# A transformer block on one Trainium2 core: arithmetic of the gated stage on VectorE instead of GpSimd, given out in smaller steps

## The chip, the cores and the metric

One core of a Trainium2 chip runs the kernel. The metric is device time in microseconds (us) of one execution; lower is better. The engines are called as the profile calls them: PE (TensorE, matmuls), DVE (VectorE), ACT (ScalarE), POOL (GpSimd), SP (SyncE, which issues nearly all DMAs). Each works through its own instructions in order and waits where one needs another engine's or a transfer's result.

## The reference

A block with adaptive layer norm, attention with a compressive memory, and a gated bilinear unit. S = 2048 rows, D = 512, 32 heads of 16, F = 1376:

```
mod = silu(c) @ w_mod                                  # six vectors sa, ca, ga, sb, cb, gb
h = layernorm(x) * (1 + ca) + sa
x = x + ga * attention(h, wq, wk, wv, wo, beta)        # four segments of 512 rows
h = layernorm(x) * (1 + cb) + sb
x = x + gb * (((h @ w_gate) * (h @ w_up)) @ w_down)    # the gated stage
```

Everything is f32, and the change lies in the last two lines.

## The kernel before

The attention part takes about 520 us. It is written out as one hand-made order of PE work, with generators that are advanced a step at a time between the matmuls, so that the preparation of later work is spread under them. The gated stage begins as the attention ends.

**Precision.** Each f32 operand of a matmul is split in a high part (rounded by ACT, `activation(..., AF.Copy)` into an `fp32r` tile, whose name ends in H or h) and a low part (operand minus high part, a subtraction, name in L or l). A product is three matmuls: high by high, high by low, low by high. A "six" is such a product over two blocks of 128 along the inner dimension: six matmuls of 128 x 512 (function `six`, matmul at L1260).

**Two passes.** Pass 0 does segments 0 and 1, pass 1 segments 2 and 3. F is cut into eleven tiles f of 128 (the last of 96). Tiles 0 and 1 of pass 0 and the last tile are multiplied directly (`open0`, `close0`, `other`; names Xg, Xu, Yg, Yu, q).

**Units.** The other tiles go in pairs (i, i + 1), first for w_gate ("g"), then for w_up ("u"). A unit computes the 2 x 2 block product (two tiles of F by two segments) with seven block products instead of eight, by sums of weight blocks and differences of blocks of h. `unit` runs them in the order 2, 5, 1, 3, 6; products 7 and 4 are carried into the next unit (`tail`). PSUM banks Z, Y and X hold the sums. ACT copies a bank out (p5, p1, y, L1369), DVE adds one bank to such a copy (`add`, L1349: p1g, yg, p5g, yu, p5u, and so on), and PE goes on writing bank X only when DVE has read it. At the end of a u unit DVE multiplies gate by up (`finish`, L1345), and `split` makes mH on ACT (L1279) and mL on DVE (L1280). `down` multiplies these with w_down (PE L1317, "acc") and DVE adds the result to the row tile (L1320, "xa"); eight such products per pair stand in the queue `dq` and are taken at fixed steps.

**Preparation.** `prepare(n)` prepares unit n, two units ahead: `wprep` loads the raw weights (cr), makes four sums of blocks S (tile cs, L479 to L483) and high and low parts of seven blocks (cwH by ACT L487, cwL by POOL L488). In three steps at the end of `wprep` each high part is followed by its low part. Units of pass 0 store cwH and cwL to DRAM (`keep`); pass 1 loads them back (`fetch`) and ACT rounds them again (L416), except for its last two units, which come from raw weights. For a u unit `wdprep` loads two tiles of w_down (crd), multiplies them by gb (L1295) and splits them (L1296, L1297). `xprep` splits the last tile's weights (cwL-1, L436). `build(p)` makes the blocks of h and their differences (`comb`, tile t, POOL L1224), each with high part bH (ACT L1216) and low part bL (DVE L1217). `lnC(s)` does the norm of segment s: statistics (L565), 1/sqrt(v + eps) by Ln and Exp on ACT with one correction step on four numbers per row (POOL L581 to L585, for s = 1 on DVE), the scaling of four row tiles x (L588), the transposes by PE, and the copies by ACT (L597).

**Order.** In the gated stage the order of PE is fixed by hand: each matmul depends on the one before it (`pe`). Other instructions are placed by a scheduler when the kernel is built; `pin` keeps one behind the last PE instruction. The driving loop takes one step of `prepare` at each of the six steps of a unit:

```
    for n in range(NU):
        pr = prepare(n + 2)
        ...
        for st in (unit if nm != "x" else x_unit)(n):
            next(pr, None)
            ...
        run(pr)
```

Of the kernel before, what the change touches and what calls it, by code (L numbers as in the profile page):

```python
# [8 lines left out]
F32 = mybir.dt.float32  # L9
# [48 lines left out]
def tile_kernel(ctx, tc, x, wq, wk_, wv, wo, beta, w_gate, w_up, w_down, c, w_mod, out):  # L58
    nc = tc.nc
# [359 lines left out]
    def xprep(n, tag, pool, rpool):  # L419

        wh = pool.tile([P, 7, 2, P], F32R, tag=f"wh{tag}", name=f"cwH{n}", bufs=1)
        wl = pool.tile([P, 7, 2, P], F32R, tag=f"wl{tag}", name=f"cwL{n}", bufs=1)
        m = ft[LAST][1]
        for j, nm in enumerate("gu"):
            plain[int(n == CH), LAST, nm] = wh[:, 0:4, j], wl[:, 0:4, j]
        flat = [a.rearrange("p a b c -> p (a b c)")[:, 0:8 * P] for a in (wh, wl)]
        if n == CH:
            yield from fetch(("x", LAST), flat, wkeep)
            return
        raw = rpool.tile([P, KT, 2, P], F32, tag="raw0", name=f"cr{n}", bufs=1)  # L430
        nc.gpsimd.memset(raw[:, :, :, m:], 0.0)
        for j, w in enumerate((w_gate, w_up)):
            pin(nc.sync.dma_start(raw[:, :, j, 0:m], w.rearrange("(k p) f -> p k f", p=P)[:, :, LAST * P:]))
        yield
        act.activation(wh[:, 0:4], raw, AF.Copy)
        nc.gpsimd.tensor_sub(wl[:, 0:4], raw, wh[:, 0:4].bitcast(F32))  # L436
        yield
        keep(("x", LAST), flat, wkeep)
        yield
# [19 lines left out]
    def wprep(n, tag, pool, rpool):  # L459

        _, nm, i = units[n]
        if (nm, i) not in wkeep:
            raw = rpool.tile([P, KT, 2, P], F32, tag=f"raw{(n + 1) % 2}", name=f"cr{n}", bufs=1)
        wh = pool.tile([P, 7, 2, P], F32R, tag=f"wh{tag}", name=f"cwH{n}", bufs=1)
        wl = pool.tile([P, 7, 2, P], F32R, tag=f"wl{tag}", name=f"cwL{n}", bufs=1)
        wslot[n] = wh, wl
        if (nm, i) in wkeep:
            yield from fetch((nm, i), [a.rearrange("p a b c -> p (a b c)") for a in (wh, wl)], wkeep)
            return
        views = [w.rearrange("(k p) f -> p k f", p=P)[:, :, i * P:] for w in (w_gate, w_up)]  # L470
        gp = nc.gpsimd
        pin(nc.sync.dma_start(raw.rearrange("p k r c -> p k (r c)"), views["gu".index(nm)][:, :, 0:2 * P]))
        yield
        S = rpool.tile([P, 4, 2, P], F32, tag="ws0", name=f"cs{n}", bufs=1)

        def A(r, c):
            return raw[:, 2 * c:2 * c + 2, r]

        gp.tensor_add(S[:, 0], A(1, 0), A(1, 1))  # L479
        gp.tensor_sub(S[:, 1], S[:, 0], A(0, 0))  # L480
        yield
        gp.tensor_sub(S[:, 2], A(0, 0), A(1, 0))
        gp.tensor_sub(S[:, 3], A(0, 1), S[:, 1])  # L483
        yield
        top = raw[:, :, 0].rearrange("p (c k) f -> p c k f", c=2)
        for d, v in ((slice(4, 6), top), (6, A(1, 1)), (slice(0, 4), S)):
            act.activation(wh[:, d], v, AF.Copy)  # L487
            gp.tensor_sub(wl[:, d], v, wh[:, d].bitcast(F32))  # L488
            yield

    def wo_load(s, pool):
        rw = []
# [61 lines left out]
    def lnC(s, pool, hpool, xpool, tag, nb, bk):  # L554

        xt = []
        for t in range(4):
            a = xpool.tile([P, D], F32, tag=tag, name=f"x1_{s}_{t}", bufs=nb)
            pin(nc.sync.dma_start(a, x1d[s][t]))
            xt.append(a)  # L560
        yield 0.1
        mv = pool.tile([P, 4, 2], F32, tag="mv", name=f"cmv{s}", bufs=2)
        for t in range(4):
            st = pool.tile([P, 6], F32, tag="st", name=f"cst{s}_{t}", bufs=2)
            pin(vec.bn_stats(st, xt[t]))  # L565
            vec.bn_aggr(mv[:, t, :], st)
            yield 0.0
        sd = pool.tile([P, 4], F32, tag="sd", name=f"csd{s}", bufs=2)
        act.activation(sd, mv[:, :, 1], AF.Ln, bias=epst[:, 0:1])
        y = pool.tile([P, 4], F32, tag="y", name=f"cy{s}", bufs=2)  # L570
        act.activation(y, sd, AF.Exp, scale=-0.5)
        a = pool.tile([P, 4], F32, tag="ya", name=f"cya{s}", bufs=2)
        b = pool.tile([P, 4], F32, tag="yb", name=f"cyb{s}", bufs=2)
        if s == 1:
            vec.tensor_mul(a, y, y)
            vec.scalar_tensor_tensor(b, mv[:, :, 1], EPS, a, op0=ALU.add, op1=ALU.mult)
            vec.tensor_scalar(b, b, -0.5, 1.5, op0=ALU.mult, op1=ALU.add)
            vec.tensor_mul(y, y, b)
        else:
            eng = nc.gpsimd  # L580
            eng.tensor_mul(a, y, y)  # L581
            eng.tensor_scalar(b, mv[:, :, 1], 1.0, EPS, op0=ALU.mult, op1=ALU.add)
            eng.tensor_mul(b, b, a)
            eng.tensor_scalar(b, b, -0.5, 1.5, op0=ALU.mult, op1=ALU.add)
            eng.tensor_mul(y, y, b)  # L585
        yield 0.0
        for t in range(4):
            pin(vec.tensor_scalar(xt[t], xt[t], mv[:, t, 0:1], y[:, t:t + 1],  # L588
                                  op0=ALU.subtract, op1=ALU.mult))
            yield 0.0  # L590
        for d in range(KT):
            if d % 2 == 0:
                hfs[s, d // 2] = hpool().tile([P, 2, L], F32, tag=f"hf{s % 2}{d // 2}", name=f"chf{s}_{d // 2}", bufs=1)
            ps = bk(f"ctp{s}_{d}")
            for t in range(4):
                TP(ps[:, t * P:(t + 1) * P], xt[t][:, d * P:(d + 1) * P], ident)
            act.activation(hfs[s, d // 2][:, d % 2], ps, AF.Identity, scale=cb_c[:, d:d + 1], bias=sb_c[:, d:d + 1])  # L597
            if s == 0:
                if d % 2 == 0:
                    pieces[0, 1 + d // 2] = tuple(hpool().tile([P, 2, L], F32R, tag=f"b{x}{1 + d // 2}", name=f"b{x}0_{1 + d // 2}", bufs=1)  # L600
                                                  for x in "hl")
                hi, lo = (a[:, d % 2] for a in pieces[0, 1 + d // 2])
                h = hfs[0, d // 2][:, d % 2]
                act.activation(hi, h, AF.Copy)
                nc.gpsimd.tensor_sub(lo, h, hi.bitcast(F32))
            yield 0.45
# [602 lines left out]
    def build(p):  # L1209

        def emit(j, srcs):
            pool = bc if j < 3 else pc
            hi = pool.tile([P, 2, L], F32R, tag=f"bh{j}", name=f"bH{p}_{j}", bufs=1)
            lo = pool.tile([P, 2, L], F32R, tag=f"bl{j}", name=f"bL{p}_{j}", bufs=1)
            for k in range(2):
                pin(act.activation(hi[:, k], srcs[k], AF.Copy))  # L1216
                pin(vec.tensor_sub(lo[:, k], srcs[k], hi[:, k].bitcast(F32)))  # L1217
            pieces[p, j] = hi, lo

        T = pc.tile([P, 2, L], F32, tag="ws1", name=f"t{p}", bufs=1)  # L1220

        def comb(a, b):
            for k in range(2):
                nc.gpsimd.tensor_sub(T[:, k], a[k], b[k])  # L1224

        t = [T[:, k] for k in range(2)]
        b11, b12, b21, b22 = ([hfs[2 * p + c, r][:, k] for k in range(2)] for r in range(2) for c in range(2))
        if p > 0:
            emit(2, b21)
            yield  # L1230
        comb(b12, b11)
        yield
        if p > 0:
            emit(1, b11)
            yield
        emit(5, t)
        yield
        emit(3, b22)
        yield
        comb(b22, t)  # L1240
        yield
        emit(6, t)
        yield
        comb(b21, t)
        yield
        emit(4, t)
        yield
        comb(b22, b12)
        yield
        emit(7, t)  # L1250
        yield
# [31 lines left out]
    def wdprep(p, f, tiles=None):  # L1283
# [10 lines left out]
        yield  # L1294
        vec.tensor_mul(r, r, gbb)  # L1295
        act.activation(hi, r, AF.Copy)  # L1296
        vec.tensor_sub(lo, r, hi.bitcast(F32))  # L1297
        yield
        keep(("d", f), (hi, lo), dkeep)
# [198 lines left out]
    for w in wdp[:2]:  # L1498
        next(w)
    run(open0(0, LAST, qa[LAST]))  # L1500
    next(wdp[2])
    next(nb)
    next(pr0)
# [34 lines left out]
    for n in range(NU):  # L1538
# [4 lines left out]
        if n == CH - 1:  # L1543
            nb = build(1)
        for st in (unit if nm != "x" else x_unit)(n):
            next(pr, None)
            if n == 0:
                next(pr1, None)
                next(nb, None)
            if n == 0:  # L1550
                d(1 + st % 2 if st > 1 else 1)
            elif st in DS[nm] and n < NU - 1:
                d()
            if 1 <= n < CH - 1:
                next(lg, None)
            if n in (CH - 1, CH):
                next(nb, None)
# [37 lines left out]
```

## Time and profile before

| | |
|---|---|
| time, median of 3 runs | 901.0 us (899.87 to 902.4) |
| profiled execution | 900.34 us, of which the profile's span is 898.6 us |
| mean granted TensorE clock | 0.99 |
| PE busy from 725 to 898.6 us | 166.48 of 173.60 us |
| DMA | 141.29 MB, mean 157 GB/s |

How to read the rows shown below. A row of the page's first part gives, for each engine, busy time, share and number of instructions. A row of stages gives the stretch, its length, busy time (and number of instructions) of PE, PEld, DVE, ACT and POOL, then the granted TensorE clock as a share of full speed, the mean share of time that the DMA engines were busy, and GB/s. A group row gives line, engine, operation, output<-inputs, shapes and count, then busy time and the mean duration of one in ns, then idle time just before these instructions and what ended it. A timeline row gives start, duration, engine, line, operation and count, and in brackets the idle time before it and what ended it. A row without a bracket waited for nothing. Instructions of an engine overlap a little: the next one starts before the one ahead has ended.

### The profile page before, as it was taken

What the parts mean: (1) busy time and instruction counts of PE and PEld (TensorE: products, weight loads), DVE (VectorE), ACT (ScalarE), POOL (GpSimd) and SP (SyncE); (2) the same over time, 40 slices, a digit from 0 to 9 for tenths busy, and PEclk for the clock granted to TensorE, in tenths of its full rate; (3) what the DMA queues carried; (4) which work ended last, traced back from release to release, by engine and by line L of the source; (5) the groups of instructions that cost most, each with busy time, mean ns of one, the idle gap of its engine ahead of it and who ended that gap; (6) DMA issues with size and microseconds to landing.
All of it is one profiled execution on the core that took longest, in us unless ns stands there. A gap on an engine that the chain in (4) does not pass through costs nothing.

```text
span 898.6 us, 14447 instructions
## 1 busy us (share of the span) xinstructions
PE 852.6 (95%) x4975; PEld 600.1 (67%) x4976; DVE 647.0 (72%) x1720; ACT 496.7 (55%) x745; POOL 389.3 (43%) x521
## 2 busy tenths in 40 slices
PE   8989999999999999999999989997899989999998
PEld 5755656556665566666666666866688768888876
DVE  8698777888788877878886368884946945545544
ACT  3758767687676865777455453252434744554420
POOL 4546536565464763856235446493550300004200
PEclk9999999999999999999999999998999999999999
DMA  7555335454454545465674484763543566443012
GB/s 235 146 160 154 109 105 143 141 156 131 128 138 128 154 145 133 120 181 177 191 216 130 153 284 153 245 258 129 211 162 132 189 232 196 180 154 124 27 48 93
DMA packets 83305, 141.29 MB, mean 157 GB/s; under 512 B 11712, under 2 KB 45504, under 8 KB 83232
## 3 DMA queue, kind: packets, MB, share of 16 engines
q1 hardware_dynamic: 83088, 140.35, 49.6%
q8 instruction: 39, 0.64, 0.3%
q14 instruction: 34, 0.28, 0.1%
q10 hardware_dynamic: 144, 0.02, 0.0%
HBM read 90.52 MB, written 49.55 MB: 156 GB/s over the span
## 4 chain that ended last, share of the span: by engine, by line
PE 71%; DVE 15%; ACT 6%; DMA 2%; issue 2%; POOL 2%; SPq 1%; ACTq 0%; DVEq 0%; POOLq 0%
PE acc L1317 13%; PE tb L85 7%; PE q L85 6%; PE k L85 6%; PE Xg L1260 6%; DVE q L39 5%; PE Xu L1260 5%; PE wops L85 4%; PE vps L85 4%; PE Yg L1260 4%; PE Yu L1260 4%; PE kps L85 3%; PE qps L85 2%; ACT pt L332 2%; PE Zu L1260 1%
## 5 line engine op out<-in xcount | busy, mean ns | idle before, releaser
L39 DVE CUSTOM_DVE_ANT_0 q<-q,cmask 128x384 f32<-128x384 f32 (+3 forms) x512 | 246.5, 508 | 49.1 <-PE q L85 39.1
L332 ACT ACTIVATE pt<-k 128x1024 f32<-128x1024 f32 x160 | 163.8, 1024 | 64.4 <-PE k L85 63.7
L338 POOL TENSOR_SCALAR_AFFINE_SELECT pt<-pt 128x256 f32<-128x256 f32 (+1 forms) x224 | 97.3, 449 | 166.4 <-ACT pt L332 164.0
L85 PE MATMUL q<-kst,qst 96*128 96x384 bf16 (+3 forms) x512 | 101.5, 299 | 11.1 <-DVE nm L39 9.8
L1320 DVE TENSOR_TENSOR xa<-xa,acc 128x512 f32<-128x512 f32 x96 | 65.3, 683 | 59.0 <-PE acc L1317 58.8
L85 PE MATMUL k<-qst,kst 98*128 98x384 bf16 (+3 forms) x512 | 97.1, 302 | 5.0 <-ACT pt L332 4.9
L85 PE MATMUL tb<-pt,v 128*32 128x512 f32 (+3 forms) x1024 | 75.5, 436 | 0.0
L39 DVE DVE_READ_ACCUMULATOR2_ANT nm<- 128x1 f32 x512 | 72.1, 141 | 0.0
L85 PEld LDWEIGHTS <-kst 98*128 98x128 bf16 x512 | 37.7, 98 | 49.5 <-issue 43.5
L85 PEld LDWEIGHTS <-qst 96*128 96x128 bf16 x512 | 43.2, 97 | 37.7 <-issue 13.6
L1317 PE MATMUL acc<-dH,mH 128*128 128x512 f32 (+1 forms) x152 | 60.8, 400 | 3.0 <-ACT mH L1279 3.0
L1317 PE MATMUL acc<-dH,mL 128*128 128x512 f32 (+1 forms) x152 | 60.3, 397 | 3.1 <-DVE mL L1280 3.1
L1317 PE MATMUL acc<-dL,mH 128*128 128x512 f32 (+1 forms) x152 | 60.3, 397 | 0.0
L479 POOL TENSOR_TENSOR cs<-cr 128x256 f32<-128x256 f32 x10 | 8.6, 856 | 107.2 <-DMA cr<-in_w_gate_dram 102.3
L85 PEld LDWEIGHTS tb<-pt,v 128*32 128x32 f32 x1024 | 28.7, 109 | 38.6 <-issue 34.4
L364 ACT ACTIVATE tsb<-tb 128x512 f32<-128x512 f32 x32 | 19.0, 595 | 41.0 <-PE tb L85 41.0
L488 POOL TENSOR_TENSOR cwL<-cr,cwH 128x512 fp32r<-128x512 f32 (+1 forms) x20 | 22.7, 1158 | 40.9 <-ACT cwH L487 40.9
L1317 PEld LDWEIGHTS acc<-dH,mL 128*128 128x128 f32 (+1 forms) x152 | 28.9, 190 | 10.3 <-DVE mL L1280 3.4
L1317 PEld LDWEIGHTS acc<-dH,mH 128*128 128x128 f32 (+1 forms) x152 | 28.8, 190 | 10.2 <-ACT mH L1279 3.4
L1317 PEld LDWEIGHTS acc<-dL,mH 128*128 128x128 f32 (+1 forms) x152 | 28.8, 189 | 7.1
L1260 PE MATMUL Xu<-bH,cwH 128*128 128x512 f32 (+1 forms) x68 | 27.4, 403 | 6.4 <-DVE p5u L1349 5.2
L85 PE MATMUL kps<-ahH,wkH 128*128 128x512 f32 x64 | 30.2, 472 | 0.0
(374 smaller groups left out, 2164.3 us busy)
## 6 DMA issues: line engine op xcount, KB each, us to landing
wm<-in_w_mod_dram SPq DMA_DIRECT2D x24, 256.0 KB, 4.3
kd<-k SPq DMA_DIRECT2D x16, 384.0 KB, 2.5
kst<-kd SPq DMA_DIRECT2D x32, 192.0 KB, 3.2
qd<-q SPq DMA_DIRECT2D x16, 384.0 KB, 3.1
qst<-qd SPq DMA_DIRECT2D x32, 192.0 KB, 3.7
x<-in_x_dram SPq DMA_DIRECT2D x16, 256.0 KB, 4.3
kst<-kd SPq DMA_DIRECT2D x32, 128.0 KB, 3.2
qst<-qd SPq DMA_DIRECT2D x32, 128.0 KB, 3.6
```

The costliest lines, as they stand in the source:

```text
L39: i = getattr(self.eng, name)(*a, **k)
L85: return pe(nc.tensor.matmul(*a, **k))
L332: ex = act.activation(pt, kp, AF.Exp, scale=0.25)
L338: sels[u, i] = nc.gpsimd.affine_select(w, w, pattern=[[0, w.shape[1]], [1, P]], compare_op=ALU.is_ge, fill=0.0, base=0, channel_multiplier=-1)
L364: act.activation(tsbs[u], tbs.pop(u), AF.Copy)
L479: gp.tensor_add(S[:, 0], A(1, 0), A(1, 1))
L488: gp.tensor_sub(wl[:, d], v, wh[:, d].bitcast(F32))
L1260: pe(nc.tensor.matmul(ps[0:n], a, b[:, k], start=first and c == 0, stop=last and c == 5, skip_group_check=True))
L1317: pe(nc.tensor.matmul(ps, a[0:m, t * P:(t + 1) * P], b[0:m], start=j == 0, stop=j == n - 1))
L1320: vec.tensor_add(xa, xa, ps)
```

## The change

All POOL arithmetic of the gated stage goes to DVE: the low part of `xprep`, sums and low parts of `wprep`, the differences of `comb`, the correction steps of `lnC` for segments 2 and 3. In `wprep` the order changes, too: high parts are made as early as their input is there, one or two steps before their low parts, and the high and low part of S (1024 columns) come in two halves. `wdprep` has a step more, between high and low part, and where it is driven by hand one `next` is added. For the preparation of u units the driving loop takes two steps at a time.

```diff
 # xprep
-        nc.gpsimd.tensor_sub(wl[:, 0:4], raw, wh[:, 0:4].bitcast(F32))
+        vec.tensor_sub(wl[:, 0:4], raw, wh[:, 0:4].bitcast(F32))
 # wprep
-        gp.tensor_add(S[:, 0], A(1, 0), A(1, 1))
-        gp.tensor_sub(S[:, 1], S[:, 0], A(0, 0))
-        yield
-        gp.tensor_sub(S[:, 2], A(0, 0), A(1, 0))
-        gp.tensor_sub(S[:, 3], A(0, 1), S[:, 1])
-        yield
-        top = raw[:, :, 0].rearrange("p (c k) f -> p c k f", c=2)
-        for d, v in ((slice(4, 6), top), (6, A(1, 1)), (slice(0, 4), S)):
-            act.activation(wh[:, d], v, AF.Copy)
-            gp.tensor_sub(wl[:, d], v, wh[:, d].bitcast(F32))
-            yield
+        def hi(d, v):
+            act.activation(wh[:, d], v, AF.Copy)
+
+        def lo(d, v):
+            vec.tensor_sub(wl[:, d], v, wh[:, d].bitcast(F32))
+
+        top = slice(4, 6), raw[:, :, 0].rearrange("p (c k) f -> p c k f", c=2)
+        low = 6, A(1, 1)
+        s1, s2 = ((d, S[:, d]) for d in (slice(0, 2), slice(2, 4)))
+        vec.tensor_add(S[:, 0], A(1, 0), A(1, 1))
+        vec.tensor_sub(S[:, 1], S[:, 0], A(0, 0))
+        hi(*top)
+        yield
+        vec.tensor_sub(S[:, 2], A(0, 0), A(1, 0))
+        vec.tensor_sub(S[:, 3], A(0, 1), S[:, 1])
+        hi(*low)
+        hi(*s1)
+        yield
+        lo(*top)
+        hi(*s2)
+        yield
+        lo(*low)
+        lo(*s1)
+        yield
+        lo(*s2)
+        yield
 # lnC: the correction step on DVE (four instructions) for s = 2 and 3 too
-        if s == 1:
+        if s > 0:
 # comb
-                nc.gpsimd.tensor_sub(T[:, k], a[k], b[k])
+                pin(vec.tensor_sub(T[:, k], a[k], b[k]))
 # wdprep
         act.activation(hi, r, AF.Copy)
+        yield
         vec.tensor_sub(lo, r, hi.bitcast(F32))
 # start of the gated stage, after open0 of the last tile
+    for w in wdp[:2]:
+        next(w)
 # driving loop
-            next(pr, None)
+            for _ in range(2 if n + 2 < NU and units[n + 2][1] == "u" else 1):
+                next(pr, None)
```

More of the change, by code (lines that the diff above doesn't have):

```diff
@@ L470, in wprep @@
         views = [w.rearrange("(k p) f -> p k f", p=P)[:, :, i * P:] for w in (w_gate, w_up)]
-        gp = nc.gpsimd
         pin(nc.sync.dma_start(raw.rearrange("p k r c -> p k (r c)"), views["gu".index(nm)][:, :, 0:2 * P]))
```

## The prediction

> **What bounds the kernel now.** I read the page first, then two stages, then the stalls of TensorE (PE), then the queue that they wait for.
>
> ```profile
> span 898.6 us, 14447 instructions
> ...
> PE 852.6 (95%) x4975; PEld 600.1 (67%) x4976; DVE 647.0 (72%) x1720; ACT 496.7 (55%) x745; POOL 389.3 (43%) x521
> ```
> ```profile
> core 0: us, PE busy (x) PEld busy (x) DVE busy (x) ACT busy (x) POOL busy (x), PEclk, DMA share, GB/s
> 521.00:725.00 204.00, 188.87 (x809) 148.62 (x810) 150.32 (x195) 92.16 (x153) 98.12 (x83) 0.97 0.57 199
> 725.00:898.60 173.60, 166.48 (x716) 133.88 (x714) 85.68 (x126) 67.78 (x104) 15.73 (x14) 0.99 0.36 128
> ```
> PE is the bound. The gated stage is 521 to 898.6. Almost all of GpSimd's (POOL's) work in it, 98 us, lies in its first 204 us, and there PE loses 204 - 188.87 = 15.1 us and some clock. PE's timeline gives every stall, in brackets, with what ended it:
>
> ```profile
> 539.61 0.49 PE L1317 MATMUL acc<-dHp,mH 128*128 128x512 f32 x1 [2.11 <-ACT mH L1279]
> 541.35 0.50 PE L1317 MATMUL acc<-dHp,mL 128*128 128x512 f32 x1 [1.24 <-DVE mL L1280]
> ...
> 596.63 0.50 PE L1260 MATMUL Xu<-bH,cwH 128*128 128x512 f32 x1 [0.35 <-DVE yu L1349]
> 601.84 0.50 PE L1260 MATMUL Xu<-bH,cwH 128*128 128x512 f32 x1 [0.79 <-DVE p5u L1349]
> 608.56 0.50 PE L1317 MATMUL acc<-dH,mH 128*128 128x512 f32 x1 [2.98 <-ACT mH L1279]
> 612.19 0.79 PE L1317 MATMUL acc<-dH,mL 128*128 128x512 f32 x1 [3.13 <-DVE mL L1280]
> 646.34 0.50 PE L1260 MATMUL Xu<-bH,cwH 128*128 128x512 f32 x1 [2.81 <-DVE p5u L1349]
> 711.29 0.50 PE L1260 MATMUL Xu<-bH,cwH 128*128 128x512 f32 x1 [1.62 <-DVE p5u L1349]
> 734.79 0.50 PE L1260 MATMUL Yg<-bH,cwH 128*128 128x512 f32 x1 [2.38 <-ACT p5g L1369]
> 867.87 0.50 PE L1260 MATMUL Xu<-bH,cwH 128*128 128x512 f32 x1 [0.85 <-DVE yu L1349]
> ```
> 18.3 us, nearly all behind VectorE (DVE); ScalarE (ACT) delivers those mH late because a DVE product is late. Why is DVE late? Its groups by shape from 521 to 725, then one from 740 to 812, where POOL does nothing, then one of the whole run:
>
> ```profile
> L1295 DVE TENSOR_TENSOR crd<-crd,gbb 128x512 f32<-128x512 f32 x11 | 12.9, 1182 | 6.1 <-DMA crd<-in_w_down_dram 6.1
> ...
> L588 DVE TENSOR_SCALAR x<-x,cmv,cy 128x512 f32<-128x512 f32 x8 | 9.5, 1212 | 0.9 <-POOL cy L585 0.9
> ...
> L1280 DVE TENSOR_TENSOR mL<-p1g,mH 128x512 fp32r<-128x512 f32 x4 | 5.6, 1408 | 1.8 <-ACT mH L1279 1.7
> ...
> L1349 DVE TENSOR_TENSOR p5u<-Xu,p5u 128x512 f32<-128x512 f32 x4 | 2.7, 678 | 0.0
> ```
> ```profile
> L1280 DVE TENSOR_TENSOR mL<-p1g,mH 128x512 fp32r<-128x512 f32 x3 | 2.1, 687 | 0.0
> ```
> ```profile
> L39 DVE TENSOR_TENSOR orow<-tr,rd 128x256 f32<-128x256 f32 x32 | 13.6, 424 | 1.5
> ```
> The same subtraction mL takes 1.41 us in the stretch with POOL and 0.69 without. An addition that reads PSUM (p5u) takes 0.68 beside POOL too. So instructions whose inputs all lie in SBUF are held up while POOL works: 12.9 - 11 x 0.69 = 5.3 us for crd alone. In the timeline one instruction can pay for a whole POOL instruction:
>
> ```profile
> 597.10 0.68 DVE L1345 TENSOR_TENSOR yg<-yg,yu 128x512 f32<-128x512 f32 x1
> 597.70 2.89 DVE L1295 TENSOR_TENSOR crd<-crd,gbb 128x512 f32<-128x512 f32 x1
> ...
> 603.46 3.26 DVE L588 TENSOR_SCALAR x<-x,cmv,cy 128x512 f32<-128x512 f32 x3
> ...
> 607.76 2.58 DVE L588 TENSOR_SCALAR x<-x,cmv,cy 128x512 f32<-128x512 f32 x1
> ...
> 646.93 0.54 DVE L588 TENSOR_SCALAR x<-x,cmv,cy 128x512 f32<-128x512 f32 x1
> ```
> Unhindered, DVE starts an instruction of 512 elements every 0.60 us (597.10, 597.70), 0.08 less than it lasts. That is my price; 256 elements come to 0.424 - 0.08 = 0.34, 1024 to 0.60 + 0.53 = 1.13, a scaling of x to 0.54 - 0.08 = 0.46 us (estimates from these rows).
>
> **The change part by part.** All arithmetic of this stage leaves POOL. *Work for DVE:* a weight unit is four sums of 256 (1.36) and low parts of 512, 256 and 2 x 512 (0.60 + 0.34 + 1.20): 3.5 us. Eight units come before 725: 28.0. The 16 differences of pieces cost 16 x 0.60 = 9.6, cwL-1 1.13, eight norm steps some 0.1 each: 39.5 us more. Off goes the hold-up, about 33 us summed over all two-input groups of this stretch against 0.69 (0.54 for x); crd 5.3, x 9.5 - 8 x 0.54 = 5.2 and mL<-p1g 2.8 of it stand above. DVE's 150.3 us become 157. **In total DVE wins nothing**; what counts is where its work lies. PE's order is the same in both built programs, so I walk DVE's new order by hand past each stall.
>
> *Start.*
> ```profile
> 527.35 3.57 DVE L1295 TENSOR_TENSOR crd<-crd,gbb 128x512 f32<-128x512 f32 x2 [4.48 <-DMA crd<-in_w_down_dram]
> ...
> 539.08 1.09 DVE L1217 TENSOR_TENSOR bL<-t,bH 128x512 fp32r<-128x512 f32 x1 [1.23 <-ACT bH L1216]
> 540.09 1.21 DVE L1280 TENSOR_TENSOR mL<-gs,mH 128x512 fp32r<-128x512 f32 x1
> ```
> From crd at 527.35 to the end of the mL that PE waits for (541.3) the new order has 17 instructions of 512 (10.2), five of 256 (1.7) and cwL-1 (1.1): 13.0 us, so 540.3. Gain **1.0**.
>
> *Second stall (596 to 612).*
> ```profile
> 583.00:597.00 14.00, 13.65 (x60) 10.85 (x59) 9.88 (x17) 6.86 (x13) 11.00 (x13) 1.00 0.64 221
> ```
> ```profile
> 585.27 0.69 DVE L1320 TENSOR_TENSOR xa<-xa,acc 128x512 f32<-128x512 f32 x1 [0.60 <-PE acc L1317]
> ```
> ```profile
> 655.12 1.40 PE Zu L1260 x6
> ```
> DVE has 14 - 9.88 = 4.1 us idle here (third busy column), which sums and low parts now fill. With PE 1.0 earlier, xa of 585.27 ends at 584.9. Then come 14 x 0.60, 6 x 0.34 and 4 x 0.1 until yu is read, at 595.7; PE wants it at 596.63 - 0.35 - 1.0 = 595.3. Then 7 x 0.60 + 0.9: p5u is read at 600.8, wanted at 600.1. Then mL0_2_1, p1g, p5g, gs, two parts of cwL4, four scalings, a third part, the mL that PE lacks, and 1.2 of small ones: 7.2 us, 608.0. PE needs two sixes of 1.40 and four matmuls (0.23 each) after p5u and stands at 604.6. So 3.4 us of stall stay, against 2.98 + 3.13; mH is in time. PE resumes at 608.1, not 612.2; gain beyond the first: **3.1**.
>
> *Third stall (646.3).*
> ```profile
> 629.01 0.70 DVE L565 BATCH_NORM_STATS2 cst<-x 128x6 f32<-128x512 f32 x1 [2.10 <-DMA x<-x1d]
> ...
> 645.61 0.68 DVE L1349 TENSOR_TENSOR p5u<-Xu,p5u 128x512 f32<-128x512 f32 x1
> ```
> The statistics start when x has landed, which PE's last transposes allow, so they move with PE. From there to the end of p5u DVE needs 17.3 us now. In the new order it is 20 x 0.60, 4 x 0.34 and 0.5: 13.9. PE wants p5u 646.34 - 2.81 - 629.01 = 14.5 after that start. The stall goes: **2.8**. Late next is the low part mL0_5_1: gs before it waits for PE's six (14.5 + 1.4 = 15.9), and with what lies between it ends at 18.1; PE wants it at 15.9 + 1.4 + 0.9 = 18.2. Just in time.
>
> *Fourth (711.3).* The hold-up of bL and mL goes, eight differences (4.8) come, and bL1_6 still waits for ACT, which rounds fetched weights as they land: about **0.4**, between 0 and 1.6. *Fifth (734.8)* is ACT behind such a fetch, the last (867.9) lies where POOL is idle: 0.
>
> *Clock.*
> ```profile
> 608.00:617.00 9.00, 5.31 (x14) 4.07 (x15) 6.18 (x7) 2.40 (x4) 5.34 (x5) 0.62 0.62 212
> 645.00:652.00 7.00, 5.66 (x18) 4.49 (x19) 6.30 (x9) 3.63 (x6) 3.24 (x4) 0.76 0.28 104
> ...
> 731.00:738.00 7.00, 4.62 (x21) 3.43 (x20) 0.80 (x2) 5.03 (x7) 0.00 (x0) 1.00 0.72 272
> ```
> After the second and third stalls the granted clock (PEclk) is below 1, and matmuls lie up to 0.43 apart instead of 0.23: some 11 x 0.2 = 2.2 and 8 x 0.2 = 1.6 us. Around the stall of 2.38 it stays 1.00. The third loss goes with its stall: **1.6**. At the second a stall of 3.4 remains, and I take half: **1.1** (0 to 2.2). The start may give 0 to 1.7 more; I take 0.
>
> The Trainium skill, "TensorE: Matmul & The Clock Gate", section "HAM oscillation — how this bites in real kernels", asks only for no idle gap above about 3.4 us. A gap of 2.81 was followed by 0.76 here, so the trace is stricter; by the rule the second clock term would be 2.2 and the sum 1.1 larger.
>
> *Other queues.* SP's stores of cwL, with loads queued behind them, now wait for DVE; by my walk the low parts are done no later than on POOL: 0, and up to 2 us if a load comes late (rival 2). ACT's rounding in two halves costs nothing, since ACT is busy 92 of 204 us. The second step of preparation per step of a unit only brings crd forward: 0 while DVE has slack, else 0.6 each. Past 725 two units add 7 us to a DVE that is busy 86 of 174: 0.
>
> *Sum:* 1.0 + 3.1 + 2.8 + 0.4 + 1.6 + 1.1 = 10.0 us. The profiled execution took 900.34 (the span and 1.7 around it); the median of three runs is 901.0, 0.1% more. 900.3 - 10.0 = **890.3 us**.
>
> **Rivals.** (1) *DVE becomes the bound*; slower. If the hold-up has another cause than POOL (transfers, say: DMA share 0.57 before 725, 0.36 after), it stays and the added work is paid: at the start 5.8 us (cwL-1, a unit, two differences) into 1.2 idle, between 583 and 611 two units, 7.0, into 4.1: 4.6 + 2.9 later, **908**. It decides from the point where less than 2.9 us of what is held up between 583 and 611 comes free (the rows of crd and x above carry 2.2 + 1.8 + 2.0 of it). Against it: 687 and 1408 ns for one shape, and p5u at 678. The Trainium skill, "Perfetto Trace Analysis", section "Identifying the Most-Contended Engine", says to serve the engine with the highest occupancy first. That is PE here; the rule gives this change no gain, as does this rival.
>
> (2) *A landing blocks DVE.*
> ```profile
> L479 POOL TENSOR_TENSOR cs<-cr 128x256 f32<-128x256 f32 x8 | 6.8, 844 | 10.0 <-DMA cr<-in_w_gate_dram 5.2 <-DMA cr<-in_w_up_dram 4.7
> ```
> POOL waited 10 us for cr; now DVE waits in its order, with xa and p5g queued behind, and PE behind them. By my walk DVE stands about 2 us before cs5 and 1 before cs7, while PE needs nothing of it. If it does, and the second stall keeps its length, 3.1 + 1.1 + 2 are lost: **896.5**.
>
> (3) *More goes:* the second stall halves again (1.7) and the clock stays full at the start and there (1.7 + 1.1): 4.5 more, **886**.
>
> That the change does not take effect is excluded: in the built program POOL has only two fills left in this stage.
>
> **How the numbers follow.** Forecast (887 to 894) 0.55; (2) 0.2; (3) 0.1; (1) 0.15. The range leaves out most of (1) and the far side of (3): 884.5 to 899.5. A run can tell about 0.3%, 2.7 us, so faster means below 898.3. Of (2) 0.04 falls to "same", of (1) 0.03. Faster 0.81, same 0.07, slower 0.12.
>
> **What would show it.** Right: mL and crd at 0.69 everywhere from 521 to 725; POOL empty; DVE busy near 157; no wait for p5u near 636; one wait of 3 us for mL near 605. Wrong: DVE instructions still over 1 us; new PE waits for an addition that stands behind cs; a longer first wait, because cwL-1 and the sums of unit 0 delay gs.

## The result, and the profile after

The changed kernel takes **889.5 us** (median of 4 runs, 887.99 to 891.86) against 901.28 us before on the same chip (median of 4, 899.87 to 902.4): a ratio of 0.9872, 95% interval 0.9846 to 0.9898. The prediction was 890.3 us. The profiled execution took 889.4 us, 10.9 less than that of before (900.34).

The head of the page, the stretches of the gated stage (columns as in the prediction: stretch, its length, then busy time and count of PE, PEld, DVE, ACT and POOL, the granted clock, DMA share and rate), and POOL's row of 40 slices:

```profile
span 887.7 us, 14457 instructions
...
PE 849.4 (96%) x4975; PEld 599.3 (68%) x4976; DVE 656.0 (74%) x1825; ACT 496.5 (56%) x755; POOL 274.8 (31%) x424
...
POOL 4545536466555674665335500000000000000000
```
```profile
521.00:725.00 204.00, 194.17 (x846) 153.51 (x845) 156.77 (x287) 96.79 (x168) 0.00 (x0) 0.99 0.60 213
725.00:887.70 162.70, 157.97 (x679) 127.42 (x677) 88.08 (x137) 62.95 (x100) 0.00 (x0) 0.99 0.33 118
```
POOL is empty from 521 us on. DVE's busy time in the first stretch is 156.77 us (predicted 157, before 150.3) with 92 more instructions, and PE is busy 5.3 us more of the same 204. DVE's groups by shape in that stretch are all back at their unhindered length:

```profile
L1309 DVE TENSOR_TENSOR crd<-crd,gbb 128x512 f32<-128x512 f32 x11 | 7.5, 686 | 4.6 <-DMA crd<-in_w_down_dram 4.6
...
L602 DVE TENSOR_SCALAR x<-x,cmv,cy 128x512 f32<-128x512 f32 x8 | 3.9, 546 | 0.0
...
L1294 DVE TENSOR_TENSOR mL<-p1g,mH 128x512 fp32r<-128x512 f32 x4 | 2.8, 690 | 0.0
```
The means were 1182, 1212 and 1408 ns before. The stalls on PE's timeline after the change:

```profile
538.93 0.49 PE L1332 MATMUL acc<-dHp,mH 128*128 128x512 f32 x1 [1.97 <-ACT mH L1293]
540.15 0.50 PE L1332 MATMUL acc<-dHp,mL 128*128 128x512 f32 x1 [0.72 <-DVE mL L1294]
...
593.88 0.50 PE L1274 MATMUL Xu<-bH,cwH 128*128 128x512 f32 x1 [0.39 <-DVE yu L1364]
598.91 0.50 PE L1274 MATMUL Xu<-bH,cwH 128*128 128x512 f32 x1 [0.60 <-DVE p5u L1364]
606.08 0.59 PE L1332 MATMUL acc<-dH,mL 128*128 128x512 f32 x1 [2.95 <-DVE mL L1294]
...
722.35 0.77 PE L1274 MATMUL Yg<-bH,cwH 128*128 128x512 f32 x1 [3.19 <-ACT p5g L1384]
...
856.98 0.50 PE L1274 MATMUL Xu<-bH,cwH 128*128 128x512 f32 x1 [0.85 <-DVE yu L1364]
```
They sum to 10.7 us, from 18.3. The third and the fourth stall are gone; the fifth has grown from 2.38 to 3.19. The stall that stays near 605 is, on DVE's timeline, the queue that the prediction walked, with mL last behind four scalings and a low part (x4 and x1 count the instructions of a row):

```profile
602.91 1.92 DVE L602 TENSOR_SCALAR x<-x,cmv,cy 128x512 f32<-128x512 f32 x4
604.74 0.69 DVE L482 TENSOR_TENSOR cwL<-cs,cwH 128x512 fp32r<-128x512 f32 x1
605.34 0.69 DVE L1294 TENSOR_TENSOR mL<-p5g,mH 128x512 fp32r<-128x512 f32 x1
```
And the fifth stall is ACT's order: p5g stands behind a rounding of fetched weights that waited for its transfer.

```profile
720.03 1.79 ACT L416 ACTIVATE cwL<-cwL 128x1024 fp32r<-128x1024 f32 x2 [5.72 <-DMA cwL<-keptLg]
721.72 0.58 ACT L1384 ACTIVATE p5g<-Yg 128x512 f32<-128x512 f32 x1
```
PE wanted p5g at 722.35 - 3.19 = 719.2, and the transfer had landed only at 720.0.

### The profile page after: what moved, and what is told of

Read it like the earlier page. It is cut to its first block, busy times and chain, and to the rows that moved or that the text cites. A ratio compares the mean times of both kernels' runs of the same rounds, so it can differ in the third digit from the quotient of the medians.

```text
span 887.7 us, 14457 instructions
## 1 busy us (share of the span) xinstructions
PE 849.4 (96%) x4975; PEld 599.3 (68%) x4976; DVE 656.0 (74%) x1825; ACT 496.5 (56%) x755; POOL 274.8 (31%) x424
## 4 chain that ended last, share of the span: by engine, by line
PE 76%; DVE 13%; ACT 6%; issue 2%; DMA 2%; POOL 1%; SPq 0%; ACTq 0%; POOLq 0%; DVEq 0%
PE acc L1332 13%; PE tb L85 8%; PE q L85 6%; PE k L85 6%; PE Xg L1274 6%; PE Xu L1274 6%; PE vps L85 5%; PE wops L85 5%; DVE q L39 4%; PE Yu L1274 4%; PE Yg L1274 4%; PE kps L85 3%; PE qps L85 3%; ACT pt L332 2%; PE Zu L1274 1%
## 5 line engine op out<-in xcount | busy, mean ns | idle before, releaser
L332 ACT ACTIVATE pt<-k 128x1024 f32<-128x1024 f32 x160 | 163.8, 1024 | 64.3 <-PE k L85 63.1
L85 PE MATMUL q<-kst,qst 96*128 96x384 bf16 (+3 forms) x512 | 101.6, 299 | 10.9 <-DVE nm L39 9.8
L1332 PEld LDWEIGHTS acc<-dH,mL 128*128 128x128 f32 (+1 forms) x152 | 28.7, 189 | 10.2 <-DVE mL L1294 3.5
L85 PE MATMUL wops<-woH,oH 128*128 128x512 f32 x64 | 28.3, 442 | 0.7 <-ACT oH L527 0.7
L85 PE MATMUL qps<-ahH,wqH 128*128 128x512 f32 x64 | 28.7, 449 | 0.0
```

The lines of the kernel that those rows point to most:

```text
L85: return pe(nc.tensor.matmul(*a, **k))
L332: ex = act.activation(pt, kp, AF.Exp, scale=0.25)
L1332: pe(nc.tensor.matmul(ps, a[0:m, t * P:(t + 1) * P], b[0:m], start=j == 0, stop=j == n - 1))
```

## The experiments

Theory A is that of the prediction: POOL's reads of SBUF hold up DVE, and their absence is the gain. Theory B is its rival: the finer steps and the new order bring the gain, whichever engine computes. Since the start of the gated stage varies by up to 2.5 us between executions, I compare, beside the medians, the time from its first matmul to the end of the span: 377.5 us before (898.6 - 521.1), 367.1 after (887.7 - 520.6). "Stalls" are the waits of PE of 0.3 us or more in that time.

### The order without the engine

Four kinds of work go back to POOL; steps and order of the change stay.

```
-            vec.tensor_sub(wl[:, d], v, wh[:, d].bitcast(F32))
+            nc.gpsimd.tensor_sub(wl[:, d], v, wh[:, d].bitcast(F32))
...
-                pin(vec.tensor_sub(T[:, k], a[k], b[k]))
+                pin(nc.gpsimd.tensor_sub(T[:, k], a[k], b[k]))
```


> The changed kernel with every moved operation given back to GpSimd (weight sums and low parts, differences of pieces, norm steps), while the smaller steps, the new order within the weight preparation and the doubled steps stay. Theory A (GpSimd's reading of SBUF holds up VectorE, and its absence is the gain): near the kernel before, 898 to 904 us, with low parts of 512 elements on VectorE at a mean above 1.0 us in the gated stage and VectorE busy there near 120 + 30. Theory B (the finer steps and the order are the gain, the engine is not): 888 to 892 us.

Measured: 892.09 us against 900.93 (ratio 0.9906, interval 0.9891 to 0.9921). This is theory B's number. Its first stretch and two of its groups:

```profile
521.00:725.00 204.00, 192.96 (x837) 152.23 (x837) 152.68 (x199) 94.54 (x164) 100.41 (x91) 0.97 0.60 208
```
```profile
L1309 DVE TENSOR_TENSOR crd<-crd,gbb 128x512 f32<-128x512 f32 x11 | 12.7, 1157 | 4.7 <-DMA crd<-in_w_down_dram 4.7
...
L1294 DVE TENSOR_TENSOR mL<-p1g,mH 128x512 fp32r<-128x512 f32 x4 | 4.5, 1137 | 1.0 <-ACT mH L1293 0.9
```
POOL is busy 100 us (98 before) and DVE 152.7 (150.3 before): the hold-up is all there, as theory A said, and most of the gain is there too, which it did not say. 369.3 us from the stage's start, 8.2 less than before. "Alone" means the source here and below: the scheduler makes each engine's order anew for every kernel that is built.

### The engine without the order

The kernel before, with `gp = nc.gpsimd` made `gp = vec` in wprep and the same for xprep, comb and the norm steps; old steps and old order.

> The kernel before with the same operations moved to VectorE and nothing else: old step sizes, old order, one step of preparation at a time. Theory A: 888 to 894 us, VectorE's 512-element instructions at 0.69 us in the gated stage, the waits near 541 and 636 us short. Theory B: 898 us or more, because VectorE then carries the work in the coarse order, with PE waiting behind low parts of 1024 elements (1.13 us each).

Measured: 891.33 us (ratio 0.9883, 0.9853 to 0.9914). This is theory A's number. The first stretch and PE's wait near 608:

```profile
521.00:725.00 204.00, 193.96 (x844) 152.00 (x843) 158.62 (x282) 95.04 (x158) 0.00 (x0) 0.99 0.62 215
```
```profile
608.03 0.50 PE L1317 MATMUL acc<-dH,mL 128*128 128x512 f32 x1 [1.54 <-DVE mL L1280]
```
367.6 us from the stage's start, 9.9 less than before. One expectation of theory A failed: the waits near 541 are as long as before (2.21 + 1.30 us, 2.11 + 1.24 before). With the order alone they are, too (2.13 + 1.23); only the whole change shortens them (1.97 + 0.72). So each half of the change alone brings nearly all of it, and the two do not add.

### Reads and fills on an idle GpSimd

The changed kernel, with work on POOL that nobody needs, first reading SBUF, then only writing it.

```
+        def idle(d):
+            for k in (d, d + 1, d, d + 1):
+                nc.gpsimd.tensor_sub(dmy, wl[:, k].bitcast(F32), wh[:, k].bitcast(F32))
...
         lo(*top)
+        idle(4)
```


> The changed kernel, and beside it 12 subtractions on GpSimd for each prepared weight unit of the gated stage (96 in all, 128x256, both inputs in SBUF, result in a tile that nobody reads; some 70 us of GpSimd by the 0.84 us of the kernel before). They hold no queue that anything waits for except the next reuse of the weight slots. Theory A: VectorE instructions with two SBUF inputs beside them go from 0.69 to over 1 us, VectorE busy in the stage from 157 to about 180 us, the time to 895 to 908 us. Theory B: 0.69 and 889.5 us, as without them.

Measured: 907.54 us (ratio 1.0077, 1.006 to 1.0094), 18 us above the changed kernel. First stretch, POOL's only group in it, crd on DVE, and two of PE's waits:

```profile
521.00:725.00 204.00, 184.46 (x788) 144.74 (x789) 176.46 (x281) 90.26 (x159) 101.02 (x96) 0.96 0.56 196
```
```profile
L488 POOL TENSOR_TENSOR dmy<-cwL,cwH 128x256 bf16<-128x256 f32 x96 | 101.0, 1052 | 75.8 <-DVE cwL L482 53.6 <-DVE cmv L589 12.4 <-DVE cy L601 3.0
```
```profile
L1318 DVE TENSOR_TENSOR crd<-crd,gbb 128x512 f32<-128x512 f32 x11 | 9.1, 829 | 4.7 <-DMA crd<-in_w_down_dram 4.7
```
```profile
601.22 0.79 PE L1283 MATMUL Xu<-bH,cwH 128*128 128x512 f32 x1 [4.26 <-DVE yu L1373]
...
620.06 0.79 PE L1341 MATMUL acc<-dH,mL 128*128 128x512 f32 x1 [5.44 <-DVE mL L1303]
```
DVE's busy time goes from 156.8 to 176.5 us with no work added to it, and no engine waits for a POOL instruction anywhere in the stage. Its means rise less than I wrote (crd to 829 ns, not over 1 us), since the reads lie beside only part of it.

In the second run the subtractions are fills: `nc.gpsimd.memset(dmy, 0.0)`, 12 for each group of four, started by a copy of one column.

> The changed kernel with 36 fills (128x256 of a tile that nobody reads) on GpSimd for each prepared weight unit in place of the subtractions of the run before; each group of 12 starts behind a copy of one column of the low part just made. They write SBUF and read nothing. Theory A in the form that only GpSimd's reading holds VectorE up: 888.5 to 890.5 us and 0.69 us. Theory A in the form that any GpSimd work on SBUF does: slower in proportion to their busy time, as with the subtractions (per us of GpSimd about a third of a us of VectorE). Theory B: 889.5 us.

Measured: 889.44 us (ratio 0.9878, 0.9861 to 0.9895). The same three views:

```profile
521.00:725.00 204.00, 195.38 (x855) 153.81 (x854) 159.60 (x291) 96.44 (x167) 103.08 (x312) 0.99 0.61 216
```
```profile
L489 POOL MEMSET dmy<- 128x256 bf16 x288 | 91.2, 317 | 16.6
```
```profile
L1319 DVE TENSOR_TENSOR crd<-crd,gbb 128x512 f32<-128x512 f32 x11 | 7.5, 685 | 4.7 <-DMA crd<-in_w_down_dram 4.7
```
POOL is as busy (103.1 against 101.0 us), and DVE doesn't notice. So the hold-up is real, it comes from POOL's reading of SBUF and not from its being busy, and 18 us hang on it where the work on DVE is that of the changed kernel. The Trainium skill, "SBUF — State Buffer", section "Who interferes with whom", states that rule: a VectorE instruction with two SBUF inputs contends with a GpSimd instruction that reads SBUF and not with one that only writes it. These two runs agree (829 and 685 ns for crd).

### Which part of the order

First the halves alone: the kernel before, with the low part of the sums in two POOL instructions.

```
-            gp.tensor_sub(wl[:, d], v, wh[:, d].bitcast(F32))
+            if d == slice(0, 4):
+                for q in (slice(0, 2), slice(2, 4)):
+                    gp.tensor_sub(wl[:, q], S[:, q], wh[:, q].bitcast(F32))
+            else:
+                gp.tensor_sub(wl[:, d], v, wh[:, d].bitcast(F32))
```


> The kernel before, with only the low part of the weight sums cut: two GpSimd subtractions of 512 elements instead of one of 1024; all else as before. Theory B1 (a VectorE instruction is held until the GpSimd instruction beside it ends, so that shorter GpSimd instructions shorten the hold-ups that PE sees): the 2.4 to 2.9 us instructions on VectorE shrink below 1.9 us, the stalls at 608 and 612 us shrink from 6.1 to 3 to 4.5 us, the time 893 to 897 us, with VectorE busy in the stage unchanged near 150 us. Theory B2 (the down-projection weights prepared in doubled steps, or the order inside the preparation, is the gain): 899 to 902 us.

Measured: 896.96 us (ratio 0.9946, 0.9929 to 0.9963). In the kernel before, crd at 597.70 lasted 2.89 us; the POOL instruction beside it, from POOL's timeline:

```profile
597.19 2.85 POOL L488 TENSOR_TENSOR cwL<-cs,cwH 128x1024 fp32r<-128x1024 f32 x1
```
It ends at 600.04, and crd 0.55 us later, as if it had begun only then. With halves, the longest single instruction of DVE at that place, p5g a little later, and the wait that PE keeps:

```profile
600.15 1.78 DVE L1301 TENSOR_TENSOR dL<-crd,dH 128x512 fp32r<-128x512 f32 x1
...
604.15 1.22 DVE L1349 TENSOR_TENSOR p5g<-p5g,p5u 128x512 f32<-128x512 f32 x1
```
```profile
610.66 0.51 PE L1321 MATMUL acc<-dH,mL 128*128 128x512 f32 x1 [4.07 <-DVE mL L1284]
```
These are B1's numbers: 1.78 instead of 2.89, 4.07 instead of 2.98 + 3.13, DVE busy 149.4 (150.3 before). But DVE's built order has changed with the halves. In the kernel before, p5g stands behind three scalings:

```profile
606.63 1.21 DVE L1345 TENSOR_TENSOR p5g<-p5g,p5u 128x512 f32<-128x512 f32 x1
```
With halves it stands ahead of all four, so that mH, which PE waited 2.98 us for, is no longer late. That shorter instructions on POOL make for shorter holds is shown; how much of the 4.3 us they bring, and how much this order, is not.

Then the steps of the down-projection weights alone: the kernel before, with the three edits to wdprep, the start and the driving loop.

> The kernel before, with only the steps of the down-projection weights changed as in the change: a step more between their rounding and their low part, two steps early at the start, and two steps of preparation for each step of a unit when the unit two ahead is an up unit. GpSimd's work is that of before. Theory B1 (length of the GpSimd instructions): 899 to 902 us. Theory B2 (these steps carry the gain): 890 to 895 us, with the stalls at 608 and 612 us cut.

Measured: 891.05 us (ratio 0.989, 0.9873 to 0.9906): B2's number, though POOL does the same work as before. DVE's timeline up to p5u, and PE's wait for it:

```profile
591.76 1.21 DVE L1295 TENSOR_TENSOR crd<-crd,gbb 128x512 f32<-128x512 f32 x1
...
598.55 4.32 DVE L588 TENSOR_SCALAR x<-x,cmv,cy 128x512 f32<-128x512 f32 x3 [0.37 <-POOL cy L585]
...
603.92 0.68 DVE L1350 TENSOR_TENSOR p5u<-Xu,p5u 128x512 f32<-128x512 f32 x1
```
```profile
604.66 0.80 PE L1260 MATMUL Xu<-bH,cwH 128*128 128x512 f32 x1 [4.53 <-DVE p5u L1350]
```
The scalings are still held up (4.32 us for three). But crd now stands in DVE's idle time at 591.8 (596.5 before), and in POOL's built order the correction step now stands ahead of the long low part, so that cy is there at 598.5 (600.6 before). So the scalings begin at 598.55 instead of 603.46 and stand ahead of p5u; what each of the two shifts brings is not told apart. PE waits once, 4.53 us, where it waited 0.35 + 0.79 + 2.98 + 3.13; the third stall is gone too. Last, the new order inside the preparation alone, on POOL, without these steps.

> The kernel before, with only the new order inside the preparation of a weight unit (high parts ahead, low part of the sums in two halves, six steps instead of five), all sums and low parts still on GpSimd and the down-projection weights prepared as before. If the halves are what counts in it: as that run, 895 to 898 us. If the earlier high parts add to it: 891 to 894 us. If it only works together with the doubled steps: 899 us or more.

Measured: 897.75 us (ratio 0.9966, 0.9952 to 0.9981): as the halves. The earlier high parts add nothing that can be told.

### Taking the two stalls that stay

These runs start from the changed kernel; it was run again beside three of them.

> The changed kernel once more, unaltered, as the measure for the three runs beside it on this chip: 888 to 891 us, a ratio of 0.985 to 0.990 to the kernel before.

Measured: 891.93 us against 901.37 (ratio 0.9902, 0.9887 to 0.9918), a little outside what I wrote and 2.4 us above the first measure. Its profile has the same stalls as the first, all within 0.3 us of it, and half the clock behind three of them instead of two. The gain of the change is thus 9 to 12 us by the two measures.

First, the queue in front of mL at 605: the four scalings four steps later, the low parts beside them tied behind PE.

```
+        if s == 2:
+            for _ in range(4):
+                yield 0.0
         for t in range(4):
             pin(vec.tensor_scalar(xt[t], xt[t], mv[:, t, 0:1], y[:, t:t + 1],
...
-            vec.tensor_sub(wl[:, d], v, wh[:, d].bitcast(F32))
+            r = vec.tensor_sub(wl[:, d], v, wh[:, d].bitcast(F32))
+            if n == 4:
+                pin(r)
...
+        if n == 4:
+            yield
+            yield
         lo(*top)
```


> The changed kernel, with the four scalings of x in the second norm given out four steps later and the low parts of the weight unit beside them tied behind PE's order, so that the low part that PE lacked at 606.1 us stands right behind the multiplication on VectorE. Theory A (that stall is only the queue on VectorE, its half clock follows from the stall): the stall of 2.95 us goes to about 0.4, its half-clock window of 3.4 us (1.7 us of work) goes, so 4.2 us: 885.3 us. Rival (the wait moves to the rounding on ScalarE or to what stood behind): 888 us or more.

Measured: 885.74 us (ratio 0.9839, 0.982 to 0.9857), 6.2 below the changed kernel beside it. mL now stands right behind gs on DVE, and PE's wait for it is short:

```profile
604.65 0.68 DVE L1368 TENSOR_TENSOR gs<-gs,Xu 128x512 f32<-128x512 f32 x1
605.90 0.69 DVE L1302 TENSOR_TENSOR mL<-p5g,mH 128x512 fp32r<-128x512 f32 x1 [0.57 <-ACT mH L1301]
```
```profile
606.64 0.50 PE L1340 MATMUL acc<-dH,mL 128*128 128x512 f32 x1 [0.23 <-DVE mL L1302]
```
That stall was the queue on DVE. A wait of 0.73 us for the mL of a later unit is new, at 639.9. The stage takes 364.7 us (369.0 in the changed kernel beside it): 1.6 less in waits, and one half-clock stretch instead of three. Second, the rounding of all fetched weights on POOL:

```
-                act.activation(b, b.bitcast(F32), AF.Copy)
+                nc.gpsimd.tensor_copy(b, b.bitcast(F32))
```


> The changed kernel, with the rounding of the weights fetched again in the second pass on GpSimd instead of ScalarE. Theory A for the stall at 722.35 us (the copy p5g stands behind a rounding that waits for its transfer): 3.19 us and the half-clock window behind it go, 4.9 us, so about 884.6 us; GpSimd reads SBUF there and holds VectorE up (0.69 to over 1 us past 700 us), which costs nothing as long as VectorE has its idle time there. Rival (the hold-ups bring new PE waits for VectorE in the second pass, or PE waits for the slower rounding): 889 us or more.

Measured: 889.87 us (ratio 0.988, 0.9864 to 0.9897), 2.1 below the changed kernel beside it, with overlapping intervals: not decided. Both edits together:

> Both edits of the two runs before together. If the two stalls are independent: 889.5 - 4.2 - 4.9 = 880.4 us. If the second one only moves when the first goes (the transfers land at their own time and PE arrives earlier): 884 to 886 us.

Measured: 885.18 us (ratio 0.9823, 0.9809 to 0.9838), the number of the second expectation, but not its mechanism. The wait for p5g is gone from both profiles, and another is there, beside POOL's copies, which read SBUF. The run with both, POOL, DVE and PE:

```profile
691.39 2.28 POOL L416 CAST cwH<-cwH 128x1024 fp32r<-128x1024 f32 x2
```
```profile
691.82 2.40 DVE L1239 TENSOR_TENSOR bL<-t,bH 128x512 fp32r<-128x512 f32 x2
```
```profile
698.85 0.50 PE L1282 MATMUL Xu<-bH,cwH 128*128 128x512 f32 x1 [1.82 <-DVE p5u L1372]
```
Two bL that take 1.29 us in the changed kernel (at 700.74) take 2.40, and the fourth stall of the kernel before is back with 1.82. So the rounding was left on ACT and one unit's put behind the copies p5g, p1g and yg, with the late scalings:

```
+                if late:
+                    tc.add_manual_dep(r.ins, copied[0].ins.name, NOSYNC, reason="order")
```
Here `late` is the one fetched unit, which also comes five steps later, and `copied[0]` is the last copy that a unit has issued.

> The changed kernel with the late scalings of before, and the rounding of one fetched weight unit (the one that p5g waited behind at 722.5 us) put behind the copies p5g, p1g and yg on ScalarE, where it stays. Theory (the stall is only the place of the rounding in ScalarE's order): the wait of 3.48 us and the half clock behind it (3.4 us at half speed, 1.7 us) go, no wait for p5u near 700 us comes in their place since GpSimd stays idle: 885.7 - 5.2 = 880.5 us. Rival (the next copy behind the rounding, p5u of the unit after, is late instead): 883.5 us or more.

Measured: 885.46 us (ratio 0.9831, 0.9804 to 0.9857): the rival's number. The stall at 722 is gone and a like one comes at the next fetched unit, though what ACT delivers late there is mH and not the copy p5u:

```profile
740.69 1.79 ACT L419 ACTIVATE cwL<-cwL 128x1024 fp32r<-128x1024 f32 x2 [3.85 <-DMA cwL<-keptLu]
742.39 0.61 ACT L1306 ACTIVATE mH<-yg 128x512 fp32r<-128x512 f32 x1
```
```profile
744.38 0.50 PE L1287 MATMUL Xu<-bH,cwH 128*128 128x512 f32 x1 [1.53 <-DVE p5u L1377]
```
mH waits behind the rounding, mL behind mH on DVE, p5u behind mL. The best version is thus the changed kernel with the late scalings, 885 to 886 us; with either cure of the fifth stall it is the same within what the runs can tell.

## Why the prediction was right, point by point

Its time, its range and its signs held; its account of where the gain is from was too narrow. Terms against the profiles, in us:

| step | predicted | measured |
|---|---|---|
| start stall | 1.0 | 3.35 - 2.69 = 0.7 |
| second stall | 3.1 | 7.25 - 3.94 = 3.3 |
| third | 2.8 | 2.8 |
| fourth | 0.4 | 1.6 |
| fifth | 0 | 2.38 - 3.19 = -0.8 |
| clock at the start | 0 (0 to 1.7) | 1.7 |
| clock behind the second | 1.1 | 2.4 - 1.7 = 0.7 |
| clock behind the third | 1.6 | 1.7 |
| clock behind the fifth | 0 | -1.7 |
| sum | 10.0 | 10.0 |

The clock rows are half of the time that PE worked in each half-clock stretch that went or came. Most of these last 3.4 us with PE at work throughout. Behind the second stall before, the stretch lasts 6.8 us, and PE stands still in the first 2.0 of them:

```profile
610.14:613.56 3.42, 1.37 (x4) 1.07 (x5) 3.32 (x6) 0.63 (x1) 1.35 (x2) 0.50 1.04 411
613.56:616.97 3.41, 3.41 (x11) 2.81 (x10) 0.69 (x2) 0.78 (x1) 1.94 (x3) 0.50 0.01 2
```
The stage became 10.4 us shorter (377.5 to 367.1); 0.4 of it is not accounted for, and another 0.5 lies ahead of the stage. In the second profile of the changed kernel the half-clock stretch at the start is there (0 instead of 1.7) and the fifth wait is 2.93 us: its rows sum to 8.5, and its stage is 8.5 us shorter than before (369.0).

That the sum comes out is in part luck. The fourth stall and the clock at the start brought 2.9 more than forecast, the fifth stall and the clock behind it took 2.5. The clock at the start belongs to the execution and not to the change: of 14 profiles 12 show that stretch, after waits of much the same length.

- **The walk of DVE's queue** was right: a wait of 2.95 us for mL at 606.1 (forecast 3.4, "one wait of 3 us for mL near 605"), none for p5u near 636, DVE at 156.8 us.
- **"The hold-up of bL and mL goes ... about 0.4"** was the term most mis-sized. The fourth stall went whole, 1.62. It stands at 1.61 or 1.62 in the kernel before and in all four others that keep the old arithmetic on POOL and is gone with the engine alone: it belongs to POOL.
- **"Fifth is ACT behind such a fetch: 0"** failed: 0.8 us are given back, and half clock behind it. SP issues this transfer behind PE's progress, so it comes earlier with PE, but not by as much. PE wants p5g 13.2 us earlier than before (732.4 to 719.2); the transfer is issued 12.2 earlier (725.3 to 713.1) and lands 12.4 earlier. How long it takes from issue to landing counts as much: about 5.2 us with the idle fills, where the wait is 0.90, 7.5 with the engine alone (2.74) and 7.1 with the late scalings (3.48). Why it takes 5 us in some executions and 7 in others is open.
- **"The second step ... only brings crd forward: 0"** holds as a term of the sum: with the engine moved already, the order adds nothing that can be told (0.9883 alone, 0.9872 and 0.9902 with it). It fails as an account of the change: on the old engine this step, with the one more in `wdprep` and the earlier start, brings 10.2 us. The prediction had no rival in which the order does it all. Hold-up and order act on the same stalls: either removes enough of what stands ahead of p5u and mL.
- **The three rivals** did not come. DVE did not become the bound, and no wait of DVE for a landing of cr reached PE. The price of the first was met in number only. With 101 us of POOL's reads beside it, the changed kernel takes 907.5 us (rival: 908), but the waits at the start, which the rival made 4.6 us longer, are 2.8 us there (2.7 without the reads); most comes at the second stall, 12.3 us of waits instead of 3.9. That PE is the busiest engine did not speak against the change either: what PE waited for was DVE's queue.

What stays open is why the part ahead of the stage varies. The two profiled executions of the changed kernel are 4.2 us apart; 2.3 of them lie ahead of the stage, and 1.9 in it, where the half-clock stretch at the start is worth 1.7.

## What to carry to other kernels

A stall of TensorE behind a queue is removed by anything that shortens or reorders the queue ahead of the awaited instruction, so two cures of one stall don't add: try each alone before either is credited. Where GpSimd reads SBUF beside VectorE, move its work; short instructions there hold VectorE for less at a time. An idle GpSimd is no free place for copies. And when PE comes earlier to a wait for a transfer, look when the transfer is issued and how long it takes: the wait can grow, and then part of the gain is given back.

## What the runs showed of the hardware that was not expected

Equal gaps of PE cost unequal clock: 2.95 and 3.19 us in the changed kernel were followed by half clock, 2.93 with the rounding on POOL and 3.48 with the late scalings were not. The traces show why. In each of the 13 profiles that have half-clock stretches while PE works in the stage, these begin and end whole multiples of 3.413 us apart, to within 0.02 us: before, they begin at 541.87, 610.14 and 647.68, which is 20 and 11 such windows. What counts is how long PE is busy in a window (the first busy time of a row, behind its length); the granted clock is the third value from the end. In the changed kernel nearly the whole gap of 2.95 us lies in one window, and the next one is at half clock:

```profile
602.94:606.35 3.41, 0.46 (x2) 0.27 (x2) 3.41 (x8) 1.16 (x3) 0.00 (x0) 1.00 0.66 269
606.35:609.78 3.43, 3.43 (x11) 2.76 (x11) 1.49 (x3) 0.78 (x1) 0.00 (x0) 0.50 0.72 228
```
With the rounding on POOL a gap of 2.93 us is split between two windows, with the late scalings one of 3.48:

```profile
607.17:610.58 3.41, 1.71 (x10) 1.45 (x11) 3.41 (x6) 0.51 (x1) 0.00 (x0) 1.00 0.62 252
610.58:614.00 3.42, 3.42 (x18) 2.83 (x17) 1.42 (x3) 0.98 (x2) 0.00 (x0) 1.00 0.97 281
```
```profile
720.67:724.08 3.41, 1.60 (x7) 1.34 (x8) 0.00 (x0) 2.52 (x4) 0.00 (x0) 1.00 0.56 216
724.08:727.50 3.42, 3.29 (x15) 2.37 (x14) 1.37 (x3) 2.00 (x4) 0.00 (x0) 1.00 0.46 160
```
Over all 14 profiles, 29 windows of the stage have PE busy for less than 1.5 us, and each is followed by a window at half clock; 1418 have it busy for more than 1.8 us, and none is. Between 1.5 and 1.8 us, 2 of 15 are. So a gap costs its clock or not by where it falls, and the place of the windows differs from one execution to the next. The Trainium skill, "TensorE: Matmul & The Clock Gate", section "What's actually happening", says that activity is watched in a free-running window of 3413 ns. The traces agree.
